# Filter load in fp32 on the hardware queue, first pair's casts by head, and a new order list, in a fused attention and FFT-gate kernel

## The chip, the cores and the metric

The kernel runs on one core of one Trainium2 chip. The metric is the device time of one execution in microseconds; the time before is the median of seven runs.

## The reference

Attention over 4 batches, 8 heads, 768 positions and head size 64, with a causal mask; five of the eight heads keep only the first 4 positions and a window of 64. Its output, as x of 4 x 768 x 512, goes through a gate with a circular convolution by FFT along the sequence:

```python
proj = x @ w_proj
x1, x2, x3 = (proj[..., :D].copy(), proj[..., D:2 * D].copy(), proj[..., 2 * D:].copy())
X2 = np.fft.rfft(x2, n=S, axis=1)
H = np.fft.rfft(filter_fft, n=S, axis=0)[None, :, :]
x2_conv = np.fft.irfft(X2 * H, n=S, axis=1)
y = x1 * x2_conv * x3
return (y @ w_out).astype(np.float32)
```

## The kernel before, in words

**Pieces.** The heads are taken in 16 pairs, n = 0 to 15, four to a batch. Every piece of work is an operation with a short name, registered with `@op`. The kernel is written out by walking through the string `ORDER` (L35 on): each word calls one operation. A word can carry an engine (`/v` VectorE, called DVE; `/s` ScalarE, ACT; `/p` GpSimd, POOL) and a slot (`@0` to `@3`). Each engine works its instructions off in the order of this list, and so do SP's queue, which issues nearly all DMAs, and POOL, which issues the converting ones. An instruction that waits holds up everything behind it on its engine. There is no other planner.

**PSUM.** All matmul results go to four slots of two banks each, tags `w0` to `w3` (`banks`, L169). A new tile in a slot waits until the readers of the one before it are done.

**A pair of heads.**
- `lq`, `lk`, `lv` (L511, L521) load Q, K and V in fp32 on SP's queue, in three sets of buffers each, so that pair n waits for the casts of pair n - 3. Rows of pairs 0 to 5 come as 1536 contiguous bytes for Q and K, all else as 256.
- `cq`, `ck`, `cv` (L182 and its neighbours in `copy`) cast to bf16. `vf` (L532, L535) makes a masked copy of V.
- For pairs 0 to 5 TensorE transposes: `Tn.0` for Q, `Tn.1` for K (L544), six transposes each, both halves of one PSUM tile, evicted by `En.0`, `En.1`. From pair 6 on `Tn` is one transpose by DMA (L554), Q and K together.
- `scn.c` (L568) are the scores in six chunks, `sb` (L581) adds a mask by a matmul for the first pairs, `ex` (L587) is the exp on ACT, `mk` (L597) multiplies by the mask on DVE for later pairs.
- `atn.0`, `atn.1` (L606) are 21 small matmuls per head; `rec`, `nm` (L616, L621) normalise on DVE.
- `f0n`, `f1n` (L628) form sum and difference of the halves of the sequence; `Sn.0`, `Sn.1` (L634) are the forward transform by matmul, evicted by `Se`. `tn` turns the output for the projection: by TensorE and `te` for pairs 0 to 3, by DMA (L656) later.

**The filter.** `lfilt` (L415) loads it on POOL's queue, converting fp32 to bf16, into `filt`, which has the bytes of tag `gy0` (as `angle` has before it). `fold0` and `fold1` (L430, L434) are sum and difference of its halves on DVE. `F0` to `F3` (L442) are its transform on TensorE, and `H...` (L452, L454) scale it into `HAB`.

**A batch.** `X` (L675) projects the spectrum with the second third of w_proj (`lw1`), `Xe`, `pa`, `pb`, `pc`, `sw` multiply by the filter, `c` (L736) transforms back, `ce`, `cv`, `y` combine. `x1`, `x3` (L711) are the other two projections (`lw0`, `lw2`), with `xs` and `g` on the other engines. `o` (L763) is the last matmul, `oe` evicts, `st` (L783, L785) stores.

**Start.** `blank` (L230) are 17 matmuls on zeros. The matrices `G` of the transform are made from `angle`, `turns`, `wrap`, `size` on DVE and four sines and cosines (L330, L336) on ACT, after which ACT loads the table for exp.

Of the kernel before, what the change touches and what calls it, by code (L numbers as in the profile page):

```python
# [9 lines left out]
FP32 = mybir.dt.float32  # L10
# [24 lines left out]
mblank tcol lq1 fcol0 table code0 blank2@0 lk0 fcol1 tfrac lret ones2 angle0/v ones0 sin0 lq0 angle2/v code1  # L35
blank1@1 lk1 quarter angle1/v lk2 blank0@0 ident lv0 unit cq1/s turns2/v lq2 turns1/v code2 turns0/v T1.0@1
ck0/s wrap0 scales lv2 E1.0/s wrap2 T0.1@0 heads0 E0.1/s wrap1 heads1@2 size sin1 lv1 cq0/v sin2 heads2 cos1
T0.0 ck1/v E0.0/v T1.1 cos2 bias1 lk3 sc0.5@0 sc0.1@2 bias0 sc0.0@3 twice01 ck2/v sb0.5 ex0.5 mask00 mask01
ex0.0 bias2 sc0.2@0 E1.1/v sb0.2 cq2/p lq3 ex0.1 T2.1@3 cv0/v sc0.4@1 lfilt sb0.4 ex0.2 vmask lv3 sc0.3@2
bias3 T2.0 mk0.0 lq4 par cv2/p ex0.4 sc1.1@0 E2.0/v lk4 sb0.3 sb1.1 ex0.3 sc1.0@1 ones1 E2.1/v vf0/p lv5  # L40
sb1.0 ex1.1 sc1.4@2 bias5 sb1.4 ck3/p at0.1@3 ex1.4 twice00 at0.0 bias4 ex1.0 cv1/v sc2.5@2 sb2.5 sc2.4@0
rec0 vf1/p lv4 ex2.5 nm0 sb2.4 sc1.3@1 ex2.4 sc1.2@2 bias6 sb1.3 cq3/p sb1.2 kinds T3.1@3 ex1.3 sc1.5@0 lw0
sb1.5 ex1.2 T3.0 sc2.3@1 E3.1/v sb2.3 ex1.5 sc2.2@2 sb2.2 ex2.3 parb mask5 at1.1@0 alt bias7 vf2/p ex2.2
E3.0/v sc2.0@1 sb2.0 at1.0 ex2.0 fold1 lq5 tn0@3 sc3.1@2 te0/s sc2.1@1 rec1 nm1 sb2.1 sb3.1 ex2.1 F2.1@3
fold0 sc3.5@0 ex3.1 sb3.5 tn1@1 F2.0 ck4/p te1/v lq6 ex3.5 f10/v sc3.3@2 lk5 H2.0/s sc3.2@1 f00/p sc3.0@0
f11/v sb3.3 sb3.2 ex3.3 sb3.0 cv3/p at2.0@3 lk6 f01/v ex3.0 at2.1 lw2 cq4/v sc3.4@2 ex3.2 sb3.4 rec2 lk7
T4.1@0 nm2 lw1 T4.0 ex3.4 S1.1@1 mask6 vf3/p S1.0 E4.0/s S0.0@2 Se1/v E4.1/s tn2@3 S0.1 mask0 te2/s mask2
sc4.1@0 sc4.0@1 f02/v at3.1@3 Se0/v ex4.0 at3.0 mask1 ex4.1 F0.1@1 f12/v lq7 rec3 cq5/v sc4.5@2 nm3 S2.0@0
ex4.5 cq6/p S2.1 f03/v tn3@3 f13/p ck5/s Se2/v sc4.2@2 F0.0 ex4.2 cv4/p lq8 te3/v S3.1@0 mk4.0 S3.0 H0.2/s
cv5/p x10.0.0@2 Se3/s H0.1/v x10.3.1@3 vf4/p H0.4/v vf5/s x10.1.1@0 H0.3/v x10.1.0 H0.0/v x10.0.1 xs0.1/s  # L50
mask3 mask4 T5.0@1 xs0.0/s ck6/v x10.3.0 lv6 T5.1 xs0.3/s x30.0.1@2 E5.1/s x30.0.0 E5.0/s X0.1.0@3 g0.0
sc5.5@1 sc5.4@0 ex5.5 sc4.4@2 X0.1.1 ex5.4 x10.2.1@1 Xe0.1/v ex4.4 x10.2.0 T6 mk5.2 sc4.3@2 xs0.2/s sc5.3@3
x30.2.1@0 mk4.2 ex5.3 cq7/p x30.2.0 lv7 ex4.3 X0.2.1@3 g0.2 ck7/s cq8/p sc5.1@2 mk4.1 sc5.0@1 T7 ex5.1
sc5.2@0 X0.2.0 ex5.2 mask7 at4.1@2 cv6/p lk8 Xe0.2/v at4.0 ex5.0 vf6/p sc6.2@0 rec4 lq9 sc6.4@3 mk5.1
X0.0.0@1 ex6.4 mk5.0 X0.0.1 ex6.2 nm4 lk10 sc6.1@3 cv7/p sc6.0@0 Xe0.0/v ex6.1 at5.1@2 vf7/p at5.0 ex6.0
f04/v sc7.1@1 sc6.5@3 rec5 ex7.1 f14/v S4.0@0 tn4 nm5 S4.1 ex6.5 sc7.4@1 mk6.0 sc7.0@2 Se4/s x30.1.0@3 ck8/v
ex7.4 twice11 T8 twice10 sc7.3@0 f05/v x30.1.1 pa0.2 ex7.3 cq9/p F3.0@1 g0.1 ex7.0 lv9 sc6.3@0 f15/p tn5
F3.1 mk6.2 ex6.3 sc7.5@2 sc7.2@3 H3.1/s F1.1@0 mk7.0 sw0.0 F1.0 mk6.1 ex7.5 ex7.2 mk7.2 lq10 at6.0@2 sw0.1
at6.1 H3.0/s mk7.1 sc8.4@3 H1.1/v at7.0@1 ex8.4 rec6 nm6 at7.1 H1.0/s S5.0@3 rec7 f16/p tn6 nm7 sc8.5@2
H1.2/s S5.1 ex8.5 f06/p S6.1@0 f17/v tn7 Se5/s sc8.0@2 sc8.3@1 f07/v ex8.0 S6.0 ck10/v lk9 S7.1@3 cv9/v lv10  # L60
ex8.3 S7.0 Se6/v vf9/p lv8 sc8.2@2 sc8.1@1 pb0.2 ex8.2 x11.0.1@0 pc0.2 Se7/s x11.0.0 lq11 pb0.1 ex8.1
x11.1.1@2 mk8.1 x31.0.0@3 cq10/s mk8.2 ck9/p x11.1.0 xs1.0/s pa0.1 x31.0.1 T9 x11.2.1@0 cv10/p g1.0 x11.2.0
x31.1.0@1 vf10/s xs1.1/v Gi cv8/p x31.1.1 X1.2.0@2 vf8/s g1.1 lk11 X1.2.1 cq11/p xs1.2/v T10 X1.1.1@1
Xe1.2/s mk8.0 pa0.0 sc9.0@0 sc9.2@3 ex9.0 sc9.3@2 pb0.0 X1.1.0 lk12 pc0.0 ex9.2 at8.0@0 Xe1.1/v at8.1 ex9.3
lv11 sc9.4@3 pc0.1 sc9.1@2 ex9.4 X1.0.0@1 mk9.1 rec8 ex9.1 X1.0.1 nm8 lq13 c0.1.0@3 mk9.0 Xe1.0/s f18/p
c0.1.1 f08/v sc10.4@0 ce0.1/s sc9.5@1 x31.2.0@2 ex10.4 ck11/p cv0.1.0 lq12 x31.2.1 cv0.1.1 ex9.5 sc10.2@3
mk9.2 sc10.5@1 c0.0.1@0 ex10.5 T11 g1.2 c0.0.0 ex10.2 S8.0@1 y0.1 S8.1 ce0.0/s cv11/v lk13 sc10.1@3 Se8/v
vf11/p at9.0@2 ex10.1 sw1.0 at9.1 cv0.0.1 cq13/p ck12/s cv0.0.0 sc10.3@3 sc10.0@1 rec9 ex10.3 mk10.2
c0.3.1@0 c0.3.0 sw1.1 nm9 ex10.0 cq12/p x30.3.1@3 ce0.3/v f19/p T12 cv0.3.1 sc11.5@1 sc11.1@2 ex11.5 f09/p
x30.3.0 cv0.3.0 ex11.1 y0.3 sc11.0@0 tn8 sc11.2@1 mk10.1 ex11.0 x11.3.1@2 g0.3 tn9 ck13/p x11.3.0 ex11.2  # L70
mk10.0 sc11.3@3 sc11.4@0 ex11.3 T13 c0.2.1@1 y0.0 c0.2.0 ex11.4 mk11.1 S9.1@3 mk11.0 lv13 S9.0 ce0.2/s lv12
xs1.3/s mk11.2 at10.0@0 cv0.2.1 at10.1 Se9/s cv0.2.0 sc12.0@2 rec10 sc12.1@3 ex12.0 nm10 at11.0@1 at11.1
ex12.1 f110/v f010/p tn10 sc12.5@2 rec11 sc12.4@0 nm11 ex12.5 S10.1@3 ex12.4 sc13.1@2 f111/v f011/p tn11
sc13.5@1 S10.0 ex13.1 S11.1@0 Se10/v lwo S11.0 lk15 ex13.5 lk14 pa1.1 sc12.2@2 Se11/s sc13.0@1 sc13.4@3
pa1.2 lq15 ex12.2 cv12/p X2.2.1@0 pb1.2 ex13.4 X2.2.0 pb1.1 ex13.0 X2.1.1@2 pa1.0 X2.1.0 Xe2.2/s pc1.2
x12.0.0@1 pb1.0 Xe2.1/s x12.0.1 mk12.2 X2.0.0@2 y0.2 xs2.0/s pc1.0 sw2.0 sc12.3@0 sc13.2@1 vf12/v ex12.3
sc13.3@3 X2.0.1 pc1.1 ex13.3 mk12.0 x12.1.0@0 Xe2.0/s mk12.1 x12.1.1 sw2.1 cv13/v c1.2.1@3 lv14 xs2.1/s
c1.1.0@2 lq14 ex13.2 c1.1.1 ck14/v lv15 c1.2.0 ce1.1/s c1.0.0@0 mk13.1 c1.0.1 cv1.1.0 cq15/p o0.2.0@1
cv1.1.1 ce1.0/s vf13/s o0.2.1 cv1.0.0 o0.3.0 cv1.0.1 o0.3.1 y1.1 c1.3.1@2 oe0.3/s y1.0 at12.0@0 mk13.2
ce1.2/s at12.1 st0.3 mk13.0 x31.3.1@1 cq14/p rec12 nm12 c1.3.0 x31.3.0 cv14/p T14 ce1.3/s cv1.2.1 ck15/s  # L80
o0.1.0@0 cv1.2.0 f112/p cv15/s o0.0.0 cv1.3.0 T15 f012/p cv1.3.1 o0.0.1 vf14/s o0.1.1 y1.3 at13.1@3 vf15/p
S12.1@2 g1.3 oe0.1/s S12.0 pa2.2 at13.0 Se12/s st0.1 pb2.1 sc14.4@0 sc14.1@1 rec13 o0.4.0@2 ex14.1 nm13
o0.4.1 o0.5.0 ex14.4 f113/v f013/p tn13 pb2.2 o0.5.1 sc14.5@3 sc14.0@1 ex14.5 x32.0.1@0 tn12 oe0.5/s pa2.0
S13.1@3 x32.0.0 y1.2 ex14.0 st0.5 S13.0 g2.0 x12.3.0@2 Se13/s pa2.1 sc15.5@0 sc14.2@1 ex15.5 x12.3.1 pc2.2
ex14.2 x32.1.0@0 xs2.3/s sc15.4@3 sc15.0@1 x32.1.1 ex15.4 x12.2.0@2 g2.1 ex15.0 o1.1.0@3 mk14.0 sc14.3@1
sc15.1@0 mk14.2 ex14.3 o1.1.1 x12.2.1 ex15.1 o1.0.0 xs2.2/v o1.0.1 sc15.2@0 oe1.1/s pb2.0 sc15.3@1 o1.3.0@2
mk14.1 ex15.2 o1.3.1 st1.1 pc2.1 o1.2.0 ex15.3 pc2.0 at14.1@3 at14.0 mk15.1 o1.2.1 mk15.2 o1.4.0@1 oe1.3/s
mk15.0 c2.1.0@0 o1.5.0 rec14 ce2.1/s nm14 at15.1@2 f014/v f114/p tn14 at15.0 c2.1.1 rec15 nm15 o1.5.1 st1.3
c2.3.0@3 c2.3.1 cv2.1.0 f115/p tn15 x32.2.0@2 cv2.1.1 f015/p o1.4.1 ce2.3/s x32.2.1 oe1.5/s S14.0@0 g2.2
S14.1 st1.5 S15.1@1 y2.1 S15.0 Se14/v c2.0.1@2 Se15/s cv2.3.1 c2.0.0 x13.1.1@0 ce2.0/v X3.2.1@1 cv2.3.0  # L90
cv2.0.0 x13.1.0 cv2.0.1 y2.3 c2.2.0@3 y2.0 c2.2.1 x13.3.0@2 ce2.2/s xs3.1/s X3.2.0 cv2.2.1 cv2.2.0 x13.2.1@0
Xe3.2/v x32.3.0@3 x32.3.1 sw3.0 sw3.1 X3.0.1@1 g2.3 X3.0.0 pa3.2 X3.1.0@3 Xe3.0/s x13.3.1 pa3.0 x13.2.0
xs3.3/s y2.2 X3.1.1 pb3.2 x33.0.1@2 pc3.2 Xe3.1/s x13.0.1@1 pb3.1 x13.0.0 pa3.1 x33.0.0 xs3.0/s pb3.0
x33.2.0@3 g3.0 x33.2.1 o2.3.0@1 pc3.1 xs3.2/s x33.1.1@2 pc3.0 g3.2 x33.1.0 o2.2.0 g3.1 c3.1.0@3 c3.1.1
o2.3.1 ce3.1/s c3.0.0@2 o2.2.1 cv3.1.0 o2.1.0@0 oe2.3/s cv3.1.1 c3.0.1 y3.1 o2.1.1 st2.3 ce3.0/v c3.3.0@1
o2.0.0 cv3.0.1 ce3.3/s cv3.0.0 o2.0.1 c3.2.1@3 oe2.1/s y3.0 c3.3.1 c3.2.0 cv3.3.1 st2.1 o2.4.0@0 cv3.3.0
ce3.2/s o2.5.0 y3.3 cv3.2.0 x33.3.0@1 cv3.2.1 o2.4.1 x33.3.1 y3.2 o2.5.1 g3.3 o3.2.0@3 oe2.5/s o3.4.0@2
st2.5 o3.2.1 o3.3.0@0 oe3.2/v o3.3.1 o3.4.1 st3.2 oe3.3/v o3.1.0@3 oe3.4/v o3.1.1 st3.3 o3.5.0@0 st3.4
o3.5.1 oe3.1/s o3.0.0@2 oe3.5/s st3.1 o3.0.1 st3.5 oe3.0/s st3.0
"""  # L100


def _runs(blocks):

    out = []
    for n, (j, i) in enumerate(blocks):
# [8 lines left out]
def kernel(  # L115
# [355 lines left out]
    def v_aug(n):  # L471
        return buf(f"v_aug{n % 3}", [128, NT, 2, 65], BF16)
# [360 lines left out]
```

## Time and profile before

| | us |
|---|---|
| median of 7 runs | 208.38 |
| lowest, highest | 206.0, 211.2 |
| the profiled execution | 211.2 |
| its span, first to last instruction | 209.5 |
| mean granted TensorE clock in it | 0.976 |
| PE, DVE, ACT, POOL busy | 191.6, 166.8, 148.6, 58.8 |

Time in the profile counts from the start of the span. A timeline row is start, duration, engine, line, operation and output<-input; the bracket at its end is how long the engine stood idle and what released it. A row of the waits is the total, how often, and the longest. A row of the chain is start, duration, and what ended last there. In the strips of the page each digit is one fortieth of the span in tenths.

### The profile page before, as it was taken

The numbers are of one execution on the slowest core, as the hardware profiler recorded it, in microseconds if no ns is written. First come the engines' busy times: TensorE is split into PE (matmuls) and PEld (weight loads), VectorE is DVE, ScalarE is ACT, GpSimd is POOL, SyncE is SP. The second block draws the span as 40 slices with busy tenths as digits, with TensorE's granted clock in tenths as the row PEclk, the third lists the DMA queues.
The fourth block names the chain that finished last, engine by engine and source line by source line (L and its number), as shares of the span: only waits on it lengthen the run. The fifth ranks groups of instructions, "written<-read, shape, count | busy, mean of one in ns | idle before, by whom it ended". The sixth has DMA issues, their size and how long they took to land.

```text
span 209.5 us, 4367 instructions
## 1 busy us (share of the span) xinstructions
PE 191.6 (91%) x1732; PEld 106.1 (51%) x1750; DVE 166.8 (80%) x284; ACT 148.6 (71%) x199; POOL 58.8 (28%) x80
## 2 busy tenths in 40 slices
PE   7659999959998999999878999999989999999992
PEld 2425667525454454545442654566444755555540
DVE  7798798936479989889797689799948888687970
ACT  4797999655898899789765899869598433243413
POOL 7055583082504405431263060018100130000000
PEclk9996999997999999999996999999999999999999
DMA  6999999988729899999999999999930280200437
GB/s 183 321 287 152 290 210 222 252 193 163 147 45 219 93 214 159 240 249 155 223 217 145 204 171 160 225 224 206 201 118 0 103 242 34 53 0 0 189 145 268
DMA packets 93622, 36.26 MB, mean 173 GB/s; under 512 B 84130, under 2 KB 90018, under 8 KB 93602
## 3 DMA queue, kind: packets, MB, share of 16 engines
q1 hardware_dynamic: 90706, 33.10, 75.9%
q0 software_dynamic: 2896, 2.88, 9.3%
q8 instruction: 13, 0.21, 0.5%
q14 instruction: 7, 0.06, 0.1%
HBM read 24.64 MB, written 6.29 MB: 148 GB/s over the span
## 4 chain that ended last, share of the span: by engine, by line
PE 57%; DMA 19%; ACT 11%; DVE 5%; issue 3%; SPq 3%; POOL 0%; ACTq 0%; DVEq 0%; POOLq 0%
PE x_ps L711 17%; PE X_ps L675 8%; DMA qkT<-qk_bf 7%; PE sc L568 6%; DMA qk_f<-in_q_dram 6%; PE c_ps L736 5%; DMA out_dram<-o 5%; PE att L606 5%; PE out_ps L763 5%; ACT pT L587 4%; PE S_ps L634 4%; PE blank_ps L230 3%; SPq L511 3%; ACT o L184 2%; DVE pT L597 2%
## 5 line engine op out<-in xcount | busy, mean ns | idle before, releaser
L587 ACT ACTIVATE pT<-sc 128x1024 bf16<-128x1024 f32 (+2 forms) x96 | 82.4, 924 | 12.6 <-PE sc L568 11.1
L711 PE MATMUL x_ps<-xT,wproj 128*128 128x384 bf16 x256 | 49.9, 339 | 0.8 <-ACT o L184 0.6
L711 PEld LDWEIGHTS <-wproj 128*128 128x128 bf16 x256 | 24.8, 101 | 22.0 <-issue 7.0
L568 PE MATMUL sc<-qkT 64*128 64x512 bf16 (+3 forms) x256 | 29.3, 317 | 6.0 <-DMA qkT<-qk_bf 3.4
L597 DVE TENSOR_TENSOR pT<-pT,mask 128x1024 bf16<-128x1024 bf16 x37 | 27.4, 766 | 4.8 <-ACT pT L587 4.8
L628 POOL TENSOR_TENSOR halves<-attn 128x384 bf16<-128x384 bf16 x16 | 16.0, 1008 | 43.9 <-DVE attn L621 36.7
L182 POOL CAST qk_bf<-qk_f 128x768 bf16<-128x768 f32 x16 | 15.0, 937 | 46.6 <-DMA qk_f<-in_q_dram 26.5
L606 PEld LDWEIGHTS <-pT 128*128 128x128 bf16 x672 | 22.4, 97 | 4.6 <-issue 1.4
L606 PE MATMUL att<-v_aug,pT 128*128 128x65 bf16 x352 | 23.5, 194 | 1.1 <-DVE attn L621 0.9
L763 PE MATMUL out_ps<-wout,gy 128*128 128x512 bf16 x88 | 23.1, 379 | 0.4
L675 PE MATMUL X_ps<-wproj,spectrum 128*128 128x512 bf16 x89 | 22.5, 380 | 0.4
L568 PEld LDWEIGHTS <-qkT 64*128 64x128 bf16 x256 | 10.4, 95 | 21.8 <-issue 13.2
L606 PE MATMUL att<-v_far,pT 128*128 128x65 bf16 x320 | 20.6, 193 | 0.0
L634 PE MATMUL S_ps<-G,halves 128*128 128x384 bf16 x96 | 18.3, 327 | 2.3 <-POOL halves L628 2.3
L725 DVE TENSOR_TENSOR gy<-x1s,x_ps 128x768 bf16<-128x768 bf16 x12 | 11.4, 952 | 9.7 <-PE x_ps L711 9.7
L736 PE MATMUL c_ps<-Gi,P 128*128 128x384 bf16 x96 | 18.4, 326 | 0.1
L747 DVE TENSOR_TENSOR conv<-evs,c_ps 128x384 bf16<-128x384 f32 x32 | 16.1, 548 | 2.5 <-ACT evs L184 1.9
L184 ACT COPY o<-out_ps 128x1024 f32<-128x1024 f32 (+1 forms) x12 | 10.7, 906 | 9.3 <-DMA out_dram<-o 7.2
L184 ACT COPY evs<-c_ps 128x384 f32<-128x384 f32 x13 | 6.2, 481 | 13.7 <-PE c_ps L736 9.9
L621 DVE TENSOR_TENSOR attn<-att,rec 128x768 bf16<-128x768 f32 x16 | 15.3, 955 | 0.8
L675 PEld LDWEIGHTS <-spectrum 128*128 128x128 bf16 x96 | 8.9, 98 | 11.2 <-issue 2.2
L184 ACT CAST x1s<-x_ps 128x768 bf16<-128x768 f32 x13 | 10.4, 807 | 5.5 <-PE x_ps L711 4.2
(102 smaller groups left out, 251.3 us busy)
## 6 DMA issues: line engine op xcount, KB each, us to landing
qk_f<-in_q_dram SPq DMA_DIRECT2D x16, 384.0 KB, 5.5
qk_f<-in_k_dram SPq DMA_DIRECT2D x16, 384.0 KB, 6.3
v_f<-in_v_dram SPq DMA_DIRECT2D x16, 384.0 KB, 6.4
out_dram<-o SPq DMA_DIRECT2D x9, 512.0 KB, 2.9
wproj<-in_moe_w_proj_dram POOLq DMA_DIRECT2D x3, 512.0 KB, 8.7
out_dram<-o SPq DMA_DIRECT2D x6, 256.0 KB, 2.3
Xw<-X SPq DMA_DIRECT2D x8, 128.0 KB, 4.5
filt<-in_moe_filter_fft_dram POOLq DMA_DIRECT2D x1, 768.0 KB, 10.6
```

The source lines that it names most:

```text
L184: nc.scalar.copy(out=out, in_=in_)
L568: nc.tensor.matmul(sc[:, hh, m * 128:(m + cnt) * 128], lhsT=qkT(n)[rows, 1, j * 128:(j + 1) * 128], rhs=qkT(n)[rows, 0, i * 128:(i + cnt) ...
L587: nc.scalar.activation(out=pT(n)[:, :, c, 0:w], in_=held[f"sc.{n}.{c}"][:, :, 0:w], func=AF.Exp, scale=SCALE)
L597: nc.vector.tensor_mul(near, near, which)
L606: nc.tensor.matmul(att[:, hh, 65 * i:65 * i + 65], lhsT=pT(n)[:, hh, c, 128 * m:128 * m + 128], rhs=(v_far(n) if i >= j + 2 else v_aug(n)) ...
L628: vp().tensor_tensor(halves(n)[:, r], a[:, 0:NM], a[:, NM:NT], kind)
L634: nc.tensor.matmul(ps[:, r, 0:HS], lhsT=halves(n)[:, r, m, :], rhs=G()[:, r, m].rearrange("p s f -> p (s f)"), start=(m == 0), stop=(m == ...
L675: nc.tensor.matmul(ps[:, u, :], lhsT=spectrum(b)[:, cc, r, seg * 128:seg * 128 + 128], rhs=wproj()[:, cc, DM:2 * DM], start=(cc == 0), sto ...
L711: nc.tensor.matmul(ps[:, s, 0:HS], lhsT=wproj()[:, cc, part * DM + cb * 128:part * DM + (cb + 1) * 128], rhs=xT(b)[:, cc, s * HS:s * HS + HS],
L736: nc.tensor.matmul(ps[:, r, 0:HS], lhsT=P(b)[:, t, u, ch], rhs=Gi()[:, r, :, seg, :], start=(seg == 0), stop=(seg == 2))
L747: fn(conv[:, half * HS:half * HS + HS], held[f"evs.{b}.{cb}"], held[f"c_ps.{b}.{cb}"][:, 1, 0:HS])
L763: nc.tensor.matmul(ps[:, i % 2, :], lhsT=gy(b)[:, cb, i * 128:(i + 1) * 128], rhs=wout()[:, cb, :], start=(cb == 0), stop=(cb == NC - 1))
```

## The change

1. The filter is loaded in fp32 by SP's queue, into the bytes of `HAB`, and both folds read fp32.
2. The casts of pair 0 are split by head: `cq0.0`, `cq0.1`, `ck0.0`, `ck0.1`.
3. For pairs 0 and 1 the transposes of Q and of K have a PSUM tile each.
4. `ORDER` is written anew from first word to last: positions, slots, and engines of many copies (among them `f03`, `f13`, `cq6`, six of the `vf`).

```diff
-    filt = C("filt", [128, NT, DM], BF16, "gy0")
+    filt = C("filt", [128, NT, DM], FP32, "HAB")
...
     @op("lfilt")
     def _():
-        nc.gpsimd.dma_start(out=filt(), in_=moe_filter_fft.rearrange("(t p) c -> p t c", p=128))
+        nc.sync.dma_start(out=filt(), in_=moe_filter_fft.rearrange("(t p) c -> p t c", p=128))
...
+    def turned(n, a):
+        return f"qkT_ps.{n}.{a}" if n < 2 else f"qkT_ps.{n}"
...
-            @op(f"c{letter}{n}")
-            def _(n=n, a=a):
-                src = held[f"qk_f32.{n}"][:, a].rearrange("p hh t d -> p t hh d")
-                copy(qk_bf(n)[:, a], src)
+            for hh in range(2 if n == 0 else 1):
+                @op(f"c{letter}{n}" + (f".{hh}" if n == 0 else ""))
+                def _(n=n, a=a, hh=hh):
+                    heads = slice(hh, hh + 1) if n == 0 else slice(0, 2)
+                    src = held[f"qk_f32.{n}"][:, a, heads].rearrange("p hh t d -> p t hh d")
+                    copy(qk_bf(n)[:, a, :, heads], src)
...
-                    ps = banks(f"qkT_ps.{n}", BF16)
+                    ps = banks(turned(n, a), BF16)
...
-                       held[f"qkT_ps.{n}"][:, a, 0:S].rearrange("d (t p) -> d p t", t=NT))
+                       held[turned(n, a)][:, a, 0:S].rearrange("d (t p) -> d p t", t=NT))
```

Of the order list, the stretch from the first transpose to the filter's load, before and after:

```diff
-T1.0@1 ck0/s wrap0 scales lv2 E1.0/s wrap2 T0.1@0 heads0 E0.1/s wrap1 heads1@2 size sin1 lv1 cq0/v sin2 heads2 cos1
-T0.0 ck1/v E0.0/v T1.1 cos2 bias1 lk3 sc0.5@0 sc0.1@2 bias0 sc0.0@3 twice01 ck2/v sb0.5 ex0.5 mask00 mask01
-ex0.0 bias2 sc0.2@0 E1.1/v sb0.2 cq2/p lq3 ex0.1 T2.1@3 cv0/v sc0.4@1 lfilt
+T0.0@0 wrap2 E0.0/s wrap1 ck0.0/v sin2 ck0.1/v size T0.1@0 sin1 heads0 cos1 E0.1/v
+heads1@1 ck2/p lk3 cos2 heads2 sc0.1@0 ck1/v sc0.4@1 sc0.3@2 bias0 T1.1@3 bias1 mask01 sb0.3 cq1/v sb0.4
+ex0.1 bias4 E1.1/v cq2/p lq3 ex0.4 sc0.0@0 twice11 lk5 mask00 T1.0@3 ex0.0 bias2 lv2 sc0.5@1 vmask sb0.5
+E1.0/v cv0/p lq4 ex0.3 sc0.2@0 bias3 sb0.2 mk0.0 ex0.5 sc1.0@3 sc1.1@2 ex0.2 vf0/v T2.0@1 lk4 sb1.0 T2.1
+bias5 ex1.0 sb1.1 ck3/p E2.0/v at0.0@0 ex1.1 sc1.4@3 cv1/p E2.1/v sb1.4 at0.1 ex1.4 ones2 cq3/v par sc2.2@1
+rec0 lk6 sb2.2 twice00 nm0 sc1.3@3 ex2.2 lv3 sc1.2@2 sb1.3 sb1.2 lfilt
```

On SP's queue the order around the filter is, before (the filter then being on POOL's), `lq3 lv3 lq4 lk4 lv5 lv4 lq5 lq6 lk5 lk6 lk7 lq7`; after, `lq3 lk5 lv2 lq4 lk4 lk6 lv3 lfilt lv4 lq5 lv5 lk7 lq6 lq7`. On POOL the thirds of w_proj come, before, in the order `lw0`, `lw2`, `lw1`, the first between the casts `cq3` and `vf2`; after, `lw0` follows `f11`, then come `lw1`, `cq5`, `lw2`.

## The prediction

> **What bounds the kernel now.** I read the page's busy rows first, then TensorE's (PE's) waits, then the chain, then GpSimd's (POOL's) timeline in the one stage where PE stands still. From the page:
>
> ```profile
> PE 191.6 (91%) x1732; PEld 106.1 (51%) x1750; DVE 166.8 (80%) x284; ACT 148.6 (71%) x199; POOL 58.8 (28%) x80
> ...
> PEclk9996999997999999999996999999999999999999
> DMA  6999999988729899999999999999930280200437
> ```
>
> PE is busy 191.6 of 209.5 us and both kernels give it the same matmuls. So an order of work can win only the 17.9 us in which PE is idle, and, in stages where PE is paced by another engine, some of the time in which it is counted busy but late. The DMA row is 9 almost without a break up to slice 30 (157 us): the transfers are a second bound. PEclk has three digits of 6 or 7: about 3.4 us each at half clock (near 16, 46 and 111 us), up to 1.7 us lost in each.
>
> PE's waits (total, times, longest):
>
> ```profile
> PE sc L568 <- DMA qkT<-qk_bf: 3.4, 3, 2.4
> PE S_ps L634 <- POOL halves L628: 2.3, 1, 2.3
> PE sc L568 <- ACT pT L587: 1.8, 1, 1.8
> ```
>
> The rest of the idle time is the start (1.3), two waits on copies at 7 to 11 us (1.9), 0.9 at 66 us, and the end after PE's last matmul at 205.1 us (4.4). The chain (start, us, what) places the first row:
>
> ```profile
> 94.09 6.18 DMA qkT<-qk_bf
> ...
> 103.40 7.56 DMA qkT<-qk_bf
> ```
>
> The transposes of pairs 10 and 11 by DMA were issued at 94.1 and 103.4 and PE had to wait for both. The trace's packets show why: the one hardware queue was never empty there, and T10's packets began at 96.3 and T11's at 106.6, behind loads issued earlier. The second row, on POOL:
>
> ```profile
> 42.93 0.99 POOL L182 CAST qk_bf<-qk_f 128x768 bf16<-128x768 f32 x1 [9.45 <-DMA qk_f<-in_q_dram]
> 43.88 0.90 POOL L628 TENSOR_TENSOR halves<-attn 128x384 bf16<-128x384 bf16 x1
> ```
>
> POOL stood 9.45 us at cq6, whose load came late; f13 is behind it on POOL, and S3.1 on PE waits for f13.
>
> **The change part by part.** *The sums.* The list is in program order for every engine, so I can add up what an engine must do before a mark. PE at the spacing of the chain's rows (a 128-column transpose 54 ns, 65 columns 30, 256 columns 108, 384 columns 162, 512 columns 216), ACT and DVE at the mean of each group, DMA at the trace's packets (a Q or K load of pairs 0 to 5 1.2 us, other loads 1.7, T 2.0, tn 1.05, a third of w_proj 3.5). "Lag" is time less PE's listed work. Before: lag 5.8 us at at3.1 (37.8 us), 8.4 at S3.1 (44.8), 10.1 at S7.0 (82.3), 13.6 at S11.0 (124.0), 13.9 at the end. Listed work, before / after:
>
> ```
>             PE            ACT           DVE
> at1.0    20.3 / 22.2   20.9 / 21.1   23.4 / 27.4
> at3.1    32.0 / 32.4   32.7 / 31.8   32.8 / 35.9
> S3.1     36.4 / 37.5   37.2 / 36.1   38.1 / 40.9
> S7.0     72.2 / 72.7   73.0 / 70.6   67.6 / 75.0
>
> DMA listed up to Tn, and PE listed up to the first score of pair n
> T8    65.1, 67.1 / 63.4, 68.1      T12  102.6, 105.5 / 105.9, 113.7
> T10   88.3, 89.5 / 87.7, 94.4      T13  106.7, 108.8 / 115.6, 123.6
> T11   97.2, 97.9 / 91.4, 98.2      T14  131.3, 133.1 / 128.1, 136.4
> ```
>
> *Start.* Before, ACT does two casts (0.83 each), two evictions (1.50 together), four sines and cosines (1.15 and 1.32), the table load (1.28), and the first exp begins at 12.74. After: pair 0 alone gates it. The two half casts of Q are each half of 0.83 plus some fixed cost, say 0.5, and run from the landing (4.3) to 5.3, covered by the 17 warm-up matmuls up to 7.08; without that cover they would cost 1.0. T0.0 to 7.4, E0.0 to 8.2, sines and cosines to 10.7, table load to 12.0: first exp at 12.05, 0.7 earlier. K's half casts (0.3 each, from the 0.56 row) are on DVE before size, which then ends at 7.8, before ACT wants it. Own tiles: T0.1 stands in the same slot as T0.0 and now waits for E0.0 (8.2); E0.1 (0.96) ends at 9.9 and scores by 10.7, hidden behind ACT's 12.05.
>
> *To S3.1* ACT sets the pace: busy 26.4 of the 28.3 us from 12.7 to 41. Listed work from the first exp: before 12.74 + (37.2 - 6.4) = 43.5; after 12.05 + (36.1 - 5.2) = 42.95, with PE 1.1 further, lag 5.4. That would be 3.0 less than 8.4. I do not take it all: DVE has 4 us more listed ahead of at1.0 (27.4, and about 1 us later at its start), which alone allows at1.0 at about 28.5, lag 6.3; and one half-clock stretch of before lies in its lag. Without the clock's part (two stretches, up to 3.4) before stands at 6.7 at S7.0; against 6.1 that gives -0.6, ends -3.0 and +1.5. The wait of 2.3 goes: in the new list cq6 is ACT's, long after, and f13 DVE's; what is late next is DVE.
>
> *Filter by the hardware queue.* Before: 768 packets of 1024 B written, 110.5 ns each on 16 engines, 5.3 us. A 2048 B packet on the hardware queue (the stores) took 96.7 ns: 4.6 us. So -0.7 us of transfer, and 1.0 us of issue leaves POOL. [...] the filter's packets ran from 16.1 to 23.3 while lv3's and lq4's ran beside them from 19.8 on. In one queue lv4, lq5, lv5 and lk7 now wait the whole 4.6. By listed DMA work the filter lands near 30 and lq5 near 34; T5.0 needs lq5 and its 0.83 cast at 32.7 + 6.2 = 39, F2.1 the filter at 30.5 + 6.2 = 37. By the row: nothing; [...] I take 0.
>
> *Folds from fp32.* The two rows (bf16) are 0.95 and 1.32 us. [...] the row nearest in kind, fp32 out of PSUM at 768 elements, is 0.96 [...]. So 3.5 against 2.3: +1.2 of DVE. By the bf16 row, 0. I take 1.2; fold0 ends near 36, F2.1 stands at 37: hidden, +1.2 if DVE is late there.
>
> *HAB takes the filter's bytes.* H2.0 must wait for both folds; F2 comes after them anyway. 0. gy0 is freed; its next use is far on. 0.
>
> *w_proj later.* lw0's issue moves from PE mark 16.8 to 26.5, behind f01 and f11 on POOL (0.91 each after nm1, near 28.5): issue at 30.5, 8.7 to landing by the page, 39.2. x10.1.1 wants it at 36.4 + 6.3 = 42.7. lw1 lands by 44, wanted at 47; lw2 by 49, at 51. 0.
>
> *Pairs 6 to 15.* The table's last block decides. Before, PE's work before pair 10's and 11's scores exceeds the DMA work before them by 1.2 and 0.7 us, and those are the two that waited. After, the excess is 6.7 and 7.0, later 8 and more. -3.4, the whole row; ends -4.5 (with the 0.9 at 66 us) and -2.0.
>
> *New waits.* The last cast now stands 5.3 us of PE work ahead of pair 13's scores, 6.1 and 6.5 for 14 and 15 (before 8.3, 5.5, 10.3). Cast 0.83, issue, and 3.2 to 5.4 to landing make 4.5 to 7. tn15 stands 3.6 ahead of x13 (before 5.1) against 2.8 to landing. +1.0, ends 0 and +3.
>
> *End.* Before, oe3.1 waited for the store of the buffer before it; with ACT behind it the last store is issued at 206.1, 1.0 after PE's end. After, oe2.5 is four matmul groups earlier. -0.3, ends -0.6 and +0.5.
>
> **Sum.** -0.6 - 3.4 + 1.0 - 0.3 = -3.3 us. The profiled execution is 211.2 (span 209.5 and 1.7 around it), so 207.9, span 206.2. Its three half-clock stretches put it above the median of 208.38 of the runs; from there: 205.1.
>
> **Rivals.** *Given back* (0.28): the waits for T10 and T11 turn into waits at the casts of pairs 12 to 15 and at DVE, which is given about 6 us more over the kernel (vf, cv and te moved to it). For: margins of 1 us at T13 to T15, DVE 80% busy. Against: DVE's listed work stays 4 us and more under PE's time after S7.0. New waits of 3 instead of 1: 207.2. *Both stages gain* (0.12): ACT's sum holds, lag 5.4: 2.4 more, 202.7. *Slower: the first third of w_proj* (0.10): lw0 stands behind nm1 on POOL and shares the engines with four loads; x10.1.1 stops PE, in order, with nothing behind it allowed past. Each us beyond 42.7 costs one; it cancels the gain from a landing at 46 on, and at 48.5 the time is 210.9. For: 10.3 us for the slowest load of that stage. Against: 8.3, 5.5 and 8.7 us for the three now. *The change does nothing* can't be: the two waits belong to the old list.
>
> **How the numbers follow.** Likeliest 0.50: 205.1, its own range 203.2 to 206.8. Range 202.0 to 209.0: it leaves out about half of the slower case and ends of the others. A measurement of this kernel can tell about 1% from no change, so the bounds are 206.3 and 210.5. Faster: 0.42 of the likeliest, 0.12, 0.06 of the rival "given back" = 0.60; slower: 0.06 of w_proj, 0.05 of others = 0.11; the rest 0.29 within.
>
> **What would show it.** First exp near 12.0; no wait of PE on qkT by DMA near pairs 10 and 11; S3.1 before 44 with no wait on POOL; folds 1.7 to 1.8 us; the filter in some 5 us, landing by 31. Wrong if x10.1.1 waits for w_proj, T5.0 for lq5, or sc13 to sc15 for their transposes over 2 us in all.

## The result, and the profile after

| | median us | runs | ratio to before, 95% interval |
|---|---|---|---|
| before, beside the changed kernel | 207.32 (203.33 to 212.05) | 61 | |
| changed | 204.41 (202.94 to 209.97) | 24 | 0.9933 [0.9899, 0.9966] |
| changed again, on another chip | 203.98 (202.5 to 207.03) | 6 | 0.9892 [0.9815, 0.9969] |

The kernel became faster, and both intervals lie below 1. How much depends on the reading: the medians differ by 2.9 us, the means by 2.4 (207.4 and 205.0), the ratio says 0.67% (1.4 us) and on the other chip 1.08% (2.2 us). The ratio is smaller because it leaves out the executions that are more than 1.5% above the fastest of their kernel; those of the changed kernel have a lower granted clock (0.973 to 0.982) than most of the rest. The 207.32 is of 61 executions of the same kernel whose first seven gave 208.38.

The changed kernel's profiled execution took 203.56 us, span 201.9, granted clock 0.992. Its page, with the rows that answer to those of before:

```profile
PE 187.6 (93%) x1736; PEld 105.3 (52%) x1750; DVE 175.7 (87%) x294; ACT 146.7 (73%) x188; POOL 49.7 (25%) x70
...
PEclk9996999999999999999999999999999999999999
DMA  5999699998799817999999999999885240501437
```

The idle time of PE went from 17.9 to 14.3 us, and its busy time for the same matmuls fell by 4.0; DVE carries 8.9 us more. PEclk has one dip where before had three, which accounts for up to 3.4 of the 4.0. The row of transfers has gaps early on, but from slice 17 to 28 (81 to 141 us) it is 9 as before: T10 and T11 still lie in a full stretch, and what can have changed is what stands ahead of them. PE's waits (total, times, longest):

```profile
PE sc L573 <- ACT pT L592: 1.3, 2, 1.1
...
PE sc L573 <- DVE attn L626: 1.2, 1, 1.2
...
PE sc L573 <- DVE gy L730: 0.8, 1, 0.8
PE att L611 <- DVE pT L602: 0.7, 1, 0.7
...
PE sc L573 <- DMA qkT<-qk_bf: 0.4, 1, 0.4
```

The first row of before, 3.4 us on the transposes by DMA, is 0.4, and the wait on POOL at S3.1 is gone. The transposes have not become quick, though. The chain (start, us, what):

```profile
97.90 8.21 DMA qkT<-qk_bf
```

T11 still took 8.21 us from its issue to PE's release. It was issued at 97.9 where before issued it at 103.4, and the first score of pair 11 comes 4.8 us earlier too, at 106.2 where before had it at 111.0. In the timeline PE waited there twice, first for DVE:

```profile
105.47 0.28 PE L573 MATMUL sc<-qkT 64*128 64x128 bf16 x4 [1.15 <-DVE attn L626]
106.15 0.39 PE L573 MATMUL sc<-qkT 64*128 64x512 bf16 x2 [0.40 <-DMA qkT<-qk_bf]
```

The three rows on DVE (1.2, 0.8, 0.7, together 2.7 us, at 105.5, 70.2 and 60.3 us) are new; the wait of 0.9 on DVE that before has at 67 us is gone.

**Lag** is, as in the prediction, the time of a mark less the matmul work listed before it. The profiled kernel before is an execution of its own: the first experiment runs it again. So the table already holds the profiles of the experiments; what counts is the change of lag within a stretch.

| profile | at0.0 to at9.0 | at9.0 to sc11.0 | sc11.0 to the end | at9.0 to the end |
|---|---|---|---|---|
| before | +4.2 | +3.4 | +0.1 | +3.5 |
| b_again, b_f13, b_filt (old list) | +0.3, -0.4, +0.8 | +3.2, +3.2, +2.6 | -0.9, -0.9, -0.8 | +2.3, +2.3, +1.8 |
| b_tfirst | +3.6 | 0.0 | +2.5 | +2.5 |
| b_dma | -1.1 | 0.0 | -0.3 | -0.3 |
| changed, a_again, a_filtpool (new list) | 0.0, +0.1, -0.5 | +2.0, +2.3, +2.3 | -2.0, -0.6, -2.0 | 0.0, +1.7, +0.3 |
| a_dma | 0.0 | +1.5 | -1.7 | -0.2 |
| a_late | +2.6 | +6.7 | +0.1 | +6.8 |

Up to at9.0 (about 102 us) old and new list lose the same, but for three profiles with more and one with less: before and b_tfirst, in which PE waited at S3.1; a_late, with half clock for 6.8 us from 16.3 us on; and b_dma, whose hardware queue took 137 us of 16 engines where b_again's took 157. Behind at9.0 the old list loses 2.5 on the mean of four profiles, the new one 0.7 of three: 1.8 us, the size of the measured gain. Two more profiles of the new list, a_startold and a_best, have -0.6 and +0.2 there.

### The profile page after: what moved, and what is told of

Same layout as the page of the kernel before. It is cut to its first block, busy times and chain, and to the rows that moved or that the text cites. A ratio compares the mean times of both kernels' runs of the same rounds, so it can differ in the third digit from the quotient of the medians.

```text
span 201.9 us, 4345 instructions
## 1 busy us (share of the span) xinstructions
PE 187.6 (93%) x1736; PEld 105.3 (52%) x1750; DVE 175.7 (87%) x294; ACT 146.7 (73%) x188; POOL 49.7 (25%) x70
## 4 chain that ended last, share of the span: by engine, by line
PE 69%; DVE 16%; ACT 5%; DMA 4%; issue 3%; ACTq 0%; DVEq 0%
PE x_ps L716 16%; PE out_ps L768 10%; PE X_ps L680 9%; PE c_ps L741 7%; PE att L611 7%; PE sc L573 7%; PE S_ps L639 5%; DMA qkT<-qk_bf 4%; ACT pT L592 4%; PE blank_ps L230 3%; DVE pT L602 3%; DVE attn L626 2%; PE F_ps L442 2%; DVE HAB L452 2%; PE sc L586 1%
## 5 line engine op out<-in xcount | busy, mean ns | idle before, releaser
L716 PE MATMUL x_ps<-xT,wproj 128*128 128x384 bf16 x256 | 47.3, 326 | 0.1
L716 PEld LDWEIGHTS <-wproj 128*128 128x128 bf16 x256 | 23.9, 98 | 19.3 <-issue 3.1
L573 PE MATMUL sc<-qkT 64*128 64x512 bf16 (+3 forms) x256 | 28.2, 312 | 4.9 <-ACT pT L592 1.3
L611 PEld LDWEIGHTS <-pT 128*128 128x128 bf16 x672 | 23.0, 97 | 4.5 <-DVE pT L602 1.1
L611 PE MATMUL att<-v_aug,pT 128*128 128x65 bf16 x352 | 24.1, 194 | 0.7 <-DVE pT L602 0.7
L768 PE MATMUL out_ps<-wout,gy 128*128 128x512 bf16 x89 | 22.5, 379 | 0.4 <-issue 0.2
L573 PEld LDWEIGHTS <-qkT 64*128 64x128 bf16 x256 | 10.4, 94 | 20.8 <-issue 14.2
L182 POOL CAST qk_bf<-qk_f 128x768 bf16<-128x768 f32 x11 | 10.5, 958 | 33.2 <-DMA qk_f<-in_k_dram 23.2
L741 PE MATMUL c_ps<-Gi,P 128*128 128x384 bf16 x96 | 17.9, 326 | 0.0
L184 ACT COPY o<-out_ps 128x1024 f32<-128x1024 f32 (+1 forms) x11 | 9.9, 900 | 8.2 <-PE out_ps L768 7.6
L540 POOL TENSOR_TENSOR v_far<-v_aug,vmask 128x520 bf16<-128x520 bf16 x9 | 10.4, 1155 | 15.4 <-DVE v_aug L180 12.6
L768 PEld LDWEIGHTS <-gy 128*128 128x128 bf16 x96 | 8.8, 98 | 9.9 <-issue 1.2
```

The source lines that it names most:

```text
L184: nc.scalar.copy(out=out, in_=in_)
L573: nc.tensor.matmul(sc[:, hh, m * 128:(m + cnt) * 128], lhsT=qkT(n)[rows, 1, j * 128:(j + 1) * 128], rhs=qkT(n)[rows, 0, i * 128:(i + cnt) ...
L611: nc.tensor.matmul(att[:, hh, 65 * i:65 * i + 65], lhsT=pT(n)[:, hh, c, 128 * m:128 * m + 128], rhs=(v_far(n) if i >= j + 2 else v_aug(n)) ...
L716: nc.tensor.matmul(ps[:, s, 0:HS], lhsT=wproj()[:, cc, part * DM + cb * 128:part * DM + (cb + 1) * 128], rhs=xT(b)[:, cc, s * HS:s * HS + HS],
L741: nc.tensor.matmul(ps[:, r, 0:HS], lhsT=P(b)[:, t, u, ch], rhs=Gi()[:, r, :, seg, :], start=(seg == 0), stop=(seg == 2))
L768: nc.tensor.matmul(ps[:, i % 2, :], lhsT=gy(b)[:, cb, i * 128:(i + 1) * 128], rhs=wout()[:, cb, :], start=(cb == 0), stop=(cb == NC - 1))
```

## The experiments

The theory: the gain comes from the stage of T10 and T11, because the new list asks for less transfer work ahead of those transposes, counted against matmul work. Rivals: it comes from the opening (split casts, own tiles), from S3.1, or from the filter's path. Pieces of the change were put into the old list and taken out of the new one.

**b_again: the kernel before, unchanged.**

> The kernel before, unchanged, to see how much of its profile is of one execution. Waits theory: TensorE's waits on pairs 10 and 11 transposed by DMA come again, 2.5 to 3.5 us in total, and the wait of S3.1 on POOL 1.5 to 2.5; time the same within 0.3%. Rival (the profiled execution was peculiar): under 1 us of waits on these transposes.

Measured 206.76 us, 1.0033 [0.9997, 1.0068]. PE's waits, the chain and the clock:

```profile
PE sc L568 <- DMA qkT<-qk_bf: 2.9, 2, 2.5
```

```profile
101.06 7.66 DMA qkT<-qk_bf
```

```profile
PEclk9985999999999999999996999999999999999998
```

The wait for T11 is there again and half clock follows it (the 6 in slice 22); the wait at S3.1 is not. So of the two waits that the prediction read, only the first is in each profile of the old list with its queue as it was; the second comes in some executions.

**b_f13: the wait at S3.1 made impossible.**

```diff
-ex4.5 cq6/p S2.1 f03/v tn3@3 f13/p ck5/s
+ex4.5 S2.1 f03/v tn3@3 f13/p cq6/p ck5/s
```

> Before, with cq6 moved behind f13 on POOL, nothing else. Waits theory: the 2.3 us wait of S3.1 on POOL goes, TensorE's lag at S3.1 falls by about 2; of it 1 to 2 us stay to the end, ratio 0.990 to 0.995. Rival (the stage is paced by ACT and by loads, whose late landing stops T4 to x10 next): ratio 0.998 to 1.002.

Measured 206.96, 1.0004 [0.9958, 1.0050]. PE waited 2.8 us for T10 and T11, and not at S3.1. The edit is worth nothing on the median, as the rival had it. The traces show what goes with the wait: lq6 shares its time with two thirds of w_proj on POOL's queue. Where the first of them was issued ahead of lq6 (at 30.7 against 30.9 us in before, within 0.1 us of it in b_tfirst), lq6 landed at 42.8 and 43.3 us; where lq6 was 1.8 us ahead or more (b_again, b_filt), at 36.0 and 35.8. No run fixed this order by itself.

**b_tfirst: the two transposes alone moved ahead of loads.**

```diff
-x31.1.0@1 vf10/s xs1.1/v Gi cv8/p x31.1.1 X1.2.0@2 vf8/s g1.1 lk11 X1.2.1 cq11/p xs1.2/v T10 X1.1.1@1
+x31.1.0@1 vf10/s xs1.1/v Gi cv8/p x31.1.1 X1.2.0@2 vf8/s g1.1 T10 lk11 X1.2.1 cq11/p xs1.2/v X1.1.1@1
...
-lv11 sc9.4@3 pc0.1 sc9.1@2 ex9.4 X1.0.0@1 mk9.1 rec8 ex9.1 X1.0.1 nm8 lq13 c0.1.0@3 ... ck11/p cv0.1.0 lq12
+lv11 sc9.4@3 pc0.1 sc9.1@2 ex9.4 X1.0.0@1 mk9.1 rec8 ex9.1 X1.0.1 nm8 c0.1.0@3 ... ck11/p cv0.1.0
...
-T11 g1.2
+T11 lq13 lq12 g1.2
```

> Before, with T10 one load earlier in SP's list (ahead of lk11) and T11 two loads earlier (ahead of lq13 and lq12). Waits theory: TensorE's wait on qkT by DMA falls from about 3 us to under 0.7, span 2 to 3 us shorter, ratio 0.986 to 0.990. Rival (the gain of the change is in the opening, its filter and casts): the wait goes but TensorE waits for something else within a few us, ratio 0.997 to 1.003.

Measured 207.2, 1.0074 [1.0034, 1.0114]: slower. PE's waits and, below, POOL's timeline:

```profile
PE S_ps L634 <- POOL halves L628: 3.2, 2, 2.7
...
PE x_ps L711 <- DMA xT<-attn: 1.1, 2, 0.7
...
PE att L606 <- DVE conv L747: 0.8, 1, 0.8
...
PE sc L568 <- DMA qkT<-qk_bf: 0.7, 1, 0.7
```

```profile
107.96 0.82 POOL L182 CAST qk_bf<-qk_f 128x768 bf16<-128x768 f32 x1 [2.44 <-DMA qk_f<-in_q_dram]
110.72 0.83 POOL L182 CAST qk_bf<-qk_f 128x768 bf16<-128x768 f32 x1 [1.93 <-DMA qk_f<-in_q_dram]
```

PE no longer waits for T10 and T11; the 0.7 is pair 13's, at 120.6 us. POOL stood 4.4 us for lq12 and lq13 instead; behind its casts stand f19 and f09, and S9.0 waited 0.5 for f09 at 114.1. Four more waits follow up to 129 us: 0.8 on DVE, the 0.7, and the two of x on transposes (1.1), 3.1 in all with the first. The table has the exchange: 0.0 where the old list lost 3, then +2.5 where it lost nothing. With T10 and T11 first in the queue, other transfers were the late ones. Nor is it the clock: the mean granted clock of this version's executions is 0.986, of before's beside them 0.981. (2.7 of the first row is S3.1 again.)

**b_dma and a_dma: less transfer work, the list untouched.** In both kernels Q and K of pairs 6 to 15 are read in the order of pairs 0 to 5, in packets of 1536 bytes, so that attention is computed with the positions of Q and K in those pairs in another order.

```diff
-                rows = "h (p t) d -> p h t d" if n < BY_PE else "h (t p) d -> p h t d"
+                rows = "h (p t) d -> p h t d"
```

> Before, with Q and K of pairs 6 to 15 read as 1536 contiguous bytes (so their positions stand in another order in these pairs): the same work everywhere, but 0.5 us less transfer for each of these 20 loads. Backlog theory: T10 and T11 land before TensorE wants them, the waits of 2.5 to 2.9 us go and the half-clock stretch behind them gets rare; 2 to 3.5 us faster, ratio 0.984 to 0.991. Rival (as with T10 and T11 put earlier: a wait removed there is given back): ratio 0.996 to 1.002.

> The changed kernel with the same shorter reads of Q and K in pairs 6 to 15 (positions in another order there). Backlog theory: little of the backlog is left in it, T11 lands some 2 us earlier, 0 to 1 us faster than the changed kernel, ratio to before 0.986 to 0.993. Rival (the changed kernel is as bound by transfers as before): 2 us or more faster than the changed kernel, ratio 0.979 to 0.984.

b_dma, the old list: 203.19, 0.9837 [0.9781, 0.9894]. a_dma, the new one: 203.36, 0.9853 [0.9799, 0.9907]. The hardware queue's row and PE's longest wait in b_dma:

```profile
q1 hardware_dynamic: 65106, 33.10, 68.3%
```

```profile
PE sc L568 <- ACT pT L587: 1.8, 1, 1.8
```

The same 33.10 MB take 68.3% of 200.4 us, 137 us on 16 engines, where b_again took 76.3% of 206.1, 157 us: 1.0 us less for each of the 20 loads, twice what was expected. PE waits for no transpose at all, and the old list gains more than the whole change does. With the backlog gone the two lists are equal as far as the runs tell (the intervals overlap almost wholly; the spans are 200.4 and 201.6). And in the new list the same edit saves next to nothing: the span is 201.6 where the changed kernel has 201.9, and on the same chip the new list with long reads and the one with the filter on POOL (a_filtpool) have 203.36 and 203.78. So most of what less transfer is worth to the old list, the new list had gained already.

**a_late: the backlog given back.** In the new list T11 goes behind lq12 and lk12.

```diff
-x11.2.0 T11 cv0.0.1 x31.2.0@1 cv0.3.1 vf9/p xs1.2/s cv0.3.0 x31.2.1 lq12 cv11/s lwo S8.1@3 g1.2 S8.0 lk12
+x11.2.0 cv0.0.1 x31.2.0@1 cv0.3.1 vf9/p xs1.2/s cv0.3.0 x31.2.1 lq12 cv11/s lwo S8.1@3 g1.2 S8.0 lk12 T11
```

> The changed kernel with T11 put behind lq12 and lk12 in SP's list, that is with two loads of backlog given back. Backlog theory: T11 lands 3 to 3.5 us later, TensorE waits 2.5 to 3.5 us for it, and in most executions a half-clock stretch follows; time 2.5 to 4.5 us up on the changed kernel, ratio to before 1.000 to 1.010. Rival (the gain comes from the list as a whole, waits are made up later): up by less than 1.5 us, ratio 0.992 to 0.998.

Measured 211.4, 1.0247 [1.0169, 1.0325], and 7.4 us over a_again of the same chip: the direction was right, the size about twice what was expected. PE's timeline, the chain, and the clock:

```profile
114.63 0.61 PE L573 MATMUL sc<-qkT 64*128 64x512 bf16 x2 [5.93 <-DMA qkT<-qk_bf]
```

```profile
104.79 9.79 DMA qkT<-qk_bf
```

```profile
PEclk9995899999999999999995899999999999999998
```

T11 is issued 6.9 us later than in the changed kernel's profile (104.8). Of this 3.9 is not the edit's: T10, which stands where it stood, is that much later too in this profile. The other 3.0 are the two loads now ahead, and T11 takes 1.6 longer. PE waits 5.93. Half clock of 6.8 us begins inside the wait, at 111.8; 4.0 us of it lie behind the wait and cost up to 2.0.

**b_filt and a_filtpool: the filter's path alone.** b_filt is the old list with the first part of the change only, a_filtpool the new list without it.

```diff
-    filt = C("filt", [128, NT, DM], BF16, "gy0")
+    filt = C("filt", [128, NT, DM], FP32, "HAB")
...
-        nc.gpsimd.dma_start(out=filt(), in_=moe_filter_fft.rearrange("(t p) c -> p t c", p=128))
+        nc.sync.dma_start(out=filt(), in_=moe_filter_fft.rearrange("(t p) c -> p t c", p=128))
```

> Before, with the filter alone changed: fp32, SP's queue, same place in the list, folds from fp32. Waits theory: folds 1.75 us each or more, loads behind it in the queue up to 4.6 us later; lq6 lands no earlier, the waits stay: ratio 0.998 to 1.006. Rival (the filter's path is the gain): loads of the first 45 us land 1 us or more earlier, ratio 0.990 to 0.995.

> The changed kernel with the filter alone put back: bf16, converted on POOL's queue at the same place in the list, folds from bf16. Theory now (pairs 10 to 15 no longer wait for the backlog of transfers, the filter's path is worth little): folds 1.2 us shorter or more, filter landing 1 us earlier or later, time within 0.4 us of the changed kernel, ratio to before 0.989 to 0.995. Rival (the filter's path is the gain, as before with it alone suggests at 0.9937): the gain goes, ratio 0.997 to 1.002.

b_filt: 205.87, 0.9937 [0.9902, 0.9971], in the rival's range, though PE's waits for T10 and T11 are still 2.9 and a new one of 0.8 stands at the fold:

```profile
PE sc L568 <- DMA qkT<-qk_bf: 2.9, 2, 2.4
...
PE F_ps L442 <- DVE fold L430: 0.8, 1, 0.8
```

a_filtpool: 203.78, 0.9859 [0.9811, 0.9906]; the new list without the fp32 filter is as fast as with it (0.9892 and 0.9933, the intervals overlap). So the new list doesn't need this part. Why the old list gained 0.6% by it stays open; the means differ by less (206.3 with an error of 0.4, against 206.7).

**a_startold: the opening of before.** Whole casts of pair 0 (one word for each in the list, where two stood) and one PSUM tile for Q's and K's transposes, in the new list.

```diff
-        return f"qkT_ps.{n}.{a}" if n < 2 else f"qkT_ps.{n}"
+        return f"qkT_ps.{n}"
...
-            for hh in range(2 if n == 0 else 1):
+            for hh in range(1):
```

> The changed kernel with whole casts for pair 0 and one PSUM tile for both of its transposes, list otherwise kept. Theory now: the first exp comes within 0.3 us of the changed kernel's, measured from the last warm-up matmul, since ACT's evictions, sines and table load set it; ratio to before 0.989 to 0.995. Rival (split casts and own tiles open the kernel earlier): first exp 0.5 us or more later and the time 0.5 to 1 us up, ratio 0.995 to 0.999.

Measured 205.0, 0.9979 [0.9919, 1.0038]. The first exp began 5.65 us after the start of the last warm-up matmul, as in every profile of the new list; every profile of the old list has 6.04. The opening's 0.4 us is therefore the list's, not that of the split casts or own tiles. But the ratio lies in the rival's range, so the time contradicts the first exp. PE's waits name a small price:

```profile
PE sc L573 <- ACT pT L592: 2.5, 4, 1.4
PE sc L573 <- DVE qkT L180: 1.5, 2, 1.0
```

They are 1.3 and 0.9 in the changed kernel. The whole profile is 1.0 us longer than the changed kernel's (202.9 and 201.9), but its last warm-up matmul also began 1.0 later (7.45 and 6.45), so the trace leaves nothing for the two parts. The mean over 19 runs, 205.0, is that of the changed kernel, which was not run on that chip. a_filtpool, which was and has both parts, is 1.2 us faster on the median of its 6 runs. Up to about that much for these two parts stays open.

**b_fill: keep PE busy in the wait.** Eleven idle matmuls of 512 columns in the slot of sc11.5; their sums are overwritten.

```diff
                 sc = banks(f"sc.{n}.{c}")
+                if (n, c) == (11, 5):
+                    for _ in range(11):
+                        nc.tensor.matmul(sc[:, 0, :], lhsT=wproj()[:, 0, 0:128], rhs=wproj()[:, 0, 0:512],
+                                         start=True, stop=True)
```

> Before, with eleven matmuls of 512 columns (2.4 us) on w_proj put into the slot of sc11.5 ahead of its own matmuls; their sums are overwritten. They fill the idle time of TensorE in front of pair 11's scores. Clock theory (an idle TensorE of 2.4 us is what brings the half-clock stretch at 109 to 114 us): no such stretch in the profile, 0.5 to 1.7 us faster, ratio 0.992 to 0.998. Rival (the half clock has another cause; the matmuls only delay): a stretch all the same, ratio 0.999 to 1.005.

Measured 209.43, 1.0141 [1.0058, 1.0224]. In the profile half clock behind T11 is gone:

```profile
PE sc L572 <- DMA qkT<-qk_bf: 0.5, 1, 0.5
```

```profile
PEclk9975999999999999999999999999999999999997
```

From x30.3.1 to at11.0 the lag grew by 2.1 (b_again 3.6, b_f13 3.7), 1.5 less, near the 1.7 that one stretch of half clock can cost (the idle matmuls are not counted as work here). But the lag then stays (9.0 at at15.0, 9.3 at the end), where b_again's falls from 11.4 to 10.4. Behind PE's last matmul this profile loses 1.4 us more than b_again's (5.5 and 4.1), where ACT waits for a store:

```profile
201.52 1.56 ACT L184 COPY o<-out_ps 128x512 f32<-128x512 f32 x3 [4.50 <-DMA out_dram<-o]
```

The median is 2.4 us above before's. It is not the clock, whose mean in these executions is 0.983, in before's beside them 0.976. What the other executions lost stays open. So half clock stayed away behind T11 in this one profile (in b_filt's it did so without a fill), and the fill did not pay.

**a_again and a_best.** a_again is the changed kernel unchanged, beside the others. a_best tries for more: filter on POOL, the load of w_out (`lwo`) behind sw0.1, and pb1.1 and y0.3 behind nm9, so that sc10.5 need not wait for DVE.

```diff
-ex7.1 sw0.0 mk7.1 sw0.1 at6.0@3
+ex7.1 sw0.0 mk7.1 sw0.1 lwo at6.0@3
...
-lq12 cv11/s lwo S8.1@3 ... at9.0 pb1.1 ex10.0 c0.2.1@0 y0.3 cv10/p rec9 c0.2.0 ex10.4 nm9 x30.3.0@3
+lq12 cv11/s S8.1@3 ... at9.0 ex10.0 c0.2.1@0 cv10/p rec9 c0.2.0 ex10.4 nm9 pb1.1 y0.3 x30.3.0@3
```

> The changed kernel itself, as the measure for the versions of it on the same chip. Both theories: ratio to before 0.987 to 0.995, one half-clock stretch near 15 us in its profile and none at 105 to 115; TensorE's wait on transposes by DMA under 0.8 us.

> The changed kernel with the filter back in bf16 on POOL's queue, w_out's load (lwo) put 30 us earlier, behind sw0.1, so that it does not share the engines with T11, and pb1.1 and y0.3 moved behind nm9 on VectorE. Backlog theory: T11 lands 3 us earlier, the wait of sc10.5 on nm9 (1.2 us) goes, of the rise in lag from at9.0 to sc11.0 (2.0 us) 1 to 1.5 us stay away; ratio to before 0.980 to 0.986. Rival (lag falls again by itself after pair 11, as it does from 8.0 to 5.5): within 0.3 us of the version with the filter alone put back.

a_again is in the first table; its wait for the transposes was 0.6, and against the expectation its profile has half clock at 109.1, behind a gap of only 1.24. a_best: 204.2, 0.9902 [0.9873, 0.9932]. Its waits:

```profile
PE sc L573 <- DVE conv L752: 1.2, 1, 1.2
PE S_ps L639 <- DVE halves L633: 1.0, 2, 0.7
```

The wait on nm9 and the one on the transposes are gone (lag +0.2 from at9.0 to sc11.0), and others on DVE took their place. The ratio misses the 0.980 to 0.986 that was expected. The median is 0.4 us from a_filtpool's, near what the rival said: a removed wait is made up elsewhere. No version that computes the same is faster than the changed kernel by more than the intervals. b_dma, on another computation, is beyond the first interval of the changed kernel (0.9894 against 0.9899), not beyond its second.

## Why the prediction was right, and where its sizes were off

**The bound and the waits for T10 and T11: right, smaller.** The sum took -3.4 for these waits and +1.0 for new ones. From at9.0 to the end the profiles give -1.8. Both terms were mis-sized. The removed wait is 2.8 to 2.9 us in three further profiles of the old list and 0.4 to 0.7 in the new one, so about 2.3 and not 3.4; that it goes is as predicted from the counts of listed transfer and matmul work, and b_dma, a_dma and a_late show by three ways that it is the backlog. The new waits are 2.7 us, not 1.0, though 0.9 on DVE near 65 us, which each profile of the old list has, went for them. They stood elsewhere, at DVE in at4.1, sc7 and sc10.5, in place of the casts of pairs 12 to 15, where no wait came. The rival *given back* had DVE as one of its two places and 3 us as its size. What kept the total from it was in part that lag falls again behind sc11.0 (-2.0 in two profiles), in part a term that the sum left out: half clock behind T11. Three of the four old profiles in which PE waits for T11 have a stretch there, at up to 1.7 us each, and of the six new ones with T11 in its place only a_again has. On one chip the mean granted clock is 0.986 in a_again's executions and 0.976 in before's beside them, which is worth about 2 us at most (an estimate, 0.010 of 205).

**Up to S3.1: wrong in size and in kind.** The -0.6 compared with a lag that held a wait of 2.3 at S3.1. It and the half clock behind it come in some executions only (two of the old list's six profiles, leaving b_f13's aside): b_f13 removes the wait by itself and gains nothing. At S7.0 the old profiles without it have lags of 5.9 to 7.7, the changed kernel, a_again, a_filtpool and a_dma 6.6 to 8.4: no gain shows there. (Of f03 and f13 only f13 changed its engine, from POOL to DVE.) What remains is the opening, 0.39 where 0.7 was predicted. The first exp at 12.05 came at 12.11, and the timeline shows why that hit says little:

```profile
7.51 0.80 ACT L184 COPY qkT<-qkT_ps 128x768 bf16<-128x768 bf16 x1 [2.58 <-PE qkT_ps L549]
...
10.81 1.28 ACT L592 ACT_TABLE_LOAD   x1
12.11 1.02 ACT L592 ACTIVATE pT<-sc 128x1024 bf16<-128x1024 f32 x1
```

ACT stood 2.58 us for the transposes, which stand behind the warm-up, and the start of its last matmul varies from 6.1 to 7.6 us between profiles. The forecast took the value of one, and the changed kernel's profile happens to have it 0.26 us earlier: the hit is partly luck.

**Filter, folds and w_proj: no effect, as predicted; one fold took longer than the estimate.** The filter's 768 packets took 96.6 ns each, 4.6 us of 16 engines as forecast, but spread from 25.4 to 31.4; it landed at 31.9, a little after the 31 named. (Before, they took 125.9 each and not 110.5, which is the mean with w_proj's: the saving is 1.4 us, not 0.7.) lq5 landed at 35.2 (about 34), lw0 at 40.7 (39.2), x10.1.1 ran at 42.8 (42.7) without a wait. The folds, from DVE's and POOL's timeline:

```profile
33.96 1.75 DVE L434 TENSOR_TENSOR fold<-filt 128x1536 bf16<-128x1536 f32 x1
35.22 1.17 POOL L182 CAST qk_bf<-qk_f 128x768 bf16<-128x768 f32 x1 [0.87 <-DMA qk_f<-in_q_dram]
35.63 2.38 DVE L430 TENSOR_TENSOR fold<-filt 128x1536 bf16<-128x1536 f32 x1
```

1.75 lies in the 1.7 to 1.8 that was named, an estimate of the author's, and b_filt has it for both folds. Two rows of before with the same operation on fp32 lead to it too: 0.55 us at 384 elements (L747) and 0.96 at 768 (L621), continued in a line 1.77 at 1536 (an estimate). The second here took 2.38, with POOL's casts beside it, as its bf16 form had taken 1.32 against 0.95. In b_filt POOL's cast began after the second fold had, and there the cast was drawn out, to 2.12 us from 0.83 in two others of that profile:

```profile
28.91 1.75 DVE L430 TENSOR_TENSOR fold<-filt 128x1536 bf16<-128x1536 f32 x1
29.22 2.12 POOL L182 CAST qk_bf<-qk_f 128x768 bf16<-128x768 f32 x1 [2.98 <-DMA qk_f<-in_k_dram]
```

The long rows stand beside each other, but no run took the casts away, so that one drew the other out was not shown. fold0 ended at 38, 2 us after the forecast. It is F2.0 that needs it (F2.1, named in the forecast, needs fold1 and ran at 36.6); PE took F2.0 the moment fold0 ended and had not stood still before. a_filtpool has the same lag at at3.1, so this cost nothing by then.

**The end: 0, not -0.3.** From PE's last matmul to the end of the span it is 4.3 us, 4.0 in before's.

**The total.** -3.3 was predicted; -1.4 to -2.9 was measured, as one reads it. The predicted 205.1 lies near 204.41 partly by luck: before itself, in 61 runs, has 207.32 and not 208.38, the removed wait was taken too large and the new ones too small, and less half clock, for which the sum has no term, may make up the rest. The slower rival (w_proj's first third) and *both stages gain* are excluded by the landing of lw0 and by the lag at S3.1 (6.5, not 5.4). Not one sign of being wrong came: PE waited neither at x10.1.1 nor at T5.0, and for no transpose of pairs 13 to 15.

## What to carry to other kernels

Where one queue in order feeds loads and transposes, count for each transpose the transfer work listed ahead of it and the matmul work listed ahead of its user; the pairs with the smallest difference (1.2 and 0.7 us in the prediction's table) were the ones that waited, and what helped here was a list with less transfer ahead (0.9933), or cheaper transfers (b_dma, 0.9837). Pulling the late ones ahead made others late (b_tfirst, 1.0074). And look for a wait in a second execution before it enters a sum: of the two large ones here, one came again in only one of five further profiles.

## What was not expected of the hardware

Half clock came behind short gaps. After 40 us of the span, a gap of PE of 2.3 to 2.7 us was followed within 1.5 us by 3.4 us at half clock in five of six cases (before twice, b_again, b_tfirst, b_f13; not b_filt). In a_again it began 2.0 us behind a gap of 1.24, with a second gap of 0.58 between. In a_late 6.8 us of it began inside the gap of 5.93. Counted from the start of the gap, half clock began after 2.5 to 3.8 us in all seven. So the waits of 2.3 us and more in these five cases may have cost up to 1.7 us beyond their own length (an estimate, half of the 3.4). A gap of that size was not followed by half clock each time, and what decides is open.

The scatter of the changed kernel's executions goes with the clock. Those with a granted clock of 0.988 or more have a mean of 203.5 us (10), those with 0.980 to 0.987 of 205.2 (9), those below of 207.6 (5). This is no proof of which causes which: b_tfirst (0.986 against 0.981) and b_fill (0.983 against 0.976) have a higher mean clock than before and are slower.
